# Gated attention and long convolution on one core: the convolution's operands are exchanged

## Chip, core and metric

The kernel runs on one core of a Trainium2 chip. The metric is device time in microseconds (us) of that core, from the first to the last instruction plus a small fixed part around it. Five engines work side by side, each through its own instruction stream in order: TensorE (PE), ScalarE (ACT), VectorE (DVE), GpSimd (POOL) and SyncE (SP, which here only starts DMA transfers). They meet at semaphores.

## The reference, cut to what matters

```python
S, D, H, Dh = 2048, 448, 16, 28          # one sequence
g = sigmoid((x * gate_w).sum(-1))         # one gate per position
q = (x @ wq).reshape(S, H, Dh); k = x @ wk; v = x @ wv      # one key and value for 16 heads
a = softmax(q k^T * Dh**-0.5) v  @ wo
dt = exp(log_dt)
K[d, l] = Re( sum_n C[d,n] * exp(dt[d] * A[d,n] * l) * dt[d] * B[d,n] )   # 256 complex modes
b[l, d] = sum_{m<=l} K[d, m] * u[l-m, d]  + u[l, d] * Dskip[d]            # by FFT in the reference
out = g * a + (1 - g) * b                 # A_x is both x and u
```

Attention has 16 x 2048 x 2048 exponentials. The second branch makes a filter K of 2048 taps for each of 448 channels and convolves it causally with x. All inputs and the output are bfloat16.

## The kernel before

**Attention.** There are 1024 score tiles of 128 keys by 512 (query, head) columns. They go through PSUM in sets of three and two: PE forms the scores (L1181), ACT takes the exponential of a whole set into a ring of 15 SBUF tiles (L1205), PE multiplies with the values (L1214) and accumulates 64 tiles in the bank psB. After 64 tiles `norm` moves psB to SBUF (`acc`, L1074 on ACT for the first 14 groups, L1076 on DVE for the next), gathers the denominators by three small DMAs of POOL (`denT`, `R_scratch`, `rdenB`) and multiplies on DVE (L1088). `outp` projects with wo and adds the result into O.

**Filter.** Channels come in 14 chunks of 32. For each chunk DVE builds tables of powers of the modes (`masters`, `tables`, L856 to L935), PE contracts them over the modes (`kgen`, L959), and the 64-column rows of taps are evacuated from PSUM: a DVE addition puts Dskip onto tap 0 (L969), an ACT copy moves the rest (L972). POOL then starts nine DMAs that write the taps reversed and padded into the DRAM scratch KP.

**Convolution.** A causal convolution is a product with a Toeplitz matrix. For four channels at a time `tload` (L996) reads KP with overlapping rows, each row starting one element after the one above, so that a DMA lays a Toeplitz tile of 128 partitions by 4288 columns (1072 KB) into SBUF. The partition index is 2m+h: m counts 64 shifts and h two halves of the sequence. There are 112 tiles, four for each of 28 half chunks; T has five buffers, and two further ones, in xT and tab, open for tiles 70 and 96 on. In `conv` PE holds columns of U stationary (x laid out by blocks of 64 positions and loaded once, 32-2n columns for step n, strided by the 448 channels) and streams 128 columns of the tile, with four channels side by side in four column groups (L1015). DVE scales the sum with 1-g (L1026), PE transposes it back (L1037), and DVE adds it into O (L1045).

**Order of the work.** The program is written as operations with what they read and write. `Prog.schedule` is a list scheduler: from estimated durations and priorities it picks the order of each engine's stream at build time[...]. A DMA is an operation of its issuing engine, with `free[e]` as its cost of issue (500 ns on SP, 1000 on POOL), `dmafree` as one shared transfer channel, and `extra` as added latency. `fill` then inserts matmuls with zeros into planned idle times of PE (L636, L640; L1187 in the score sets). `emit` writes waits for those dependencies that cross engines. The tile loads wait for the taps of their chunk in KP and for a free buffer; the convolution waits for its tile.

**What the change touches.** The constants NTR and `free[e]`; the buffers U, T, cst, dtb and the scratch KP in `alloc`; memsets in `consts`; the loads of U and the pad in `loads`; stores in `prep_x`; the last level in `masters`; the evacuation in `kgen`; `tload`; `conv`; and the copy at the head of `norm`.

Of the kernel before, what the change touches and what calls it, by code (L numbers as in the profile page):

```python
# [32 lines left out]
NTR = 5  # L33
# [47 lines left out]
class Prog:  # L81
# [65 lines left out]

    def schedule(self):
# [20 lines left out]
        while done < n:  # L169
# [55 lines left out]
            if o.slot is not None:  # L225
                free[e] = r + (1000.0 if e == "pool" else 500.0) * o.ndma
                s = r if e == "pool" else max(r, dmafree)
                end = s + o.ns + self.DMA_NS + o.extra
                dmafree = max(dmafree, s) + o.ns
            else:  # L230
                free[e] = r + o.ns
                end = free[e] + o.lat
# [124 lines left out]
class Kernel:  # L357
# [34 lines left out]
    def alloc(self):  # L392
# [23 lines left out]
        self.U = sb("U", D * 32, BF)  # L416
        self.O = sb("O", 16 * D, BF)
        self.T = sb("T", NTR * TW, BF)
        self.tslots = [(self.T, s * TW, ["tpdone", "rawdone"]) for s in range(NTR)]
        self.tslots.append((self.xT, NT * S - TW - 2048, [("xT", hp, q) for hp in range(2) for q in range(3)]))  # L420
        self.tmap, self.tlast = {}, [s - 9 for s in range(NTR)] + [-20, -20]
# [14 lines left out]
        self.cst = sb("cst", 512, BF)  # L436
# [4 lines left out]
        self.KP = nc.dram_tensor("KP_scratch", (2 * KH,), BF).ap()  # L441
# [4 lines left out]
    def consts(self):  # L446
# [6 lines left out]
        dm(V(self.kstg, 0, 256), 0.0, 170, [("kst", 0, 0), ("kst", 1, 0)])  # L453
# [10 lines left out]
        for k in range(2):  # L464
            dm(V(self.U, (16 + 8 * k) * D, 8 * D), 0.0, 1550, ["Uz"])
# [17 lines left out]
        dm(V(self.Wo, 0, NT * D), 0.0, 810, ["Wo"], 5)  # L483
        for q in range(4):
            dm(V(self.O, q * 4 * D, 4 * D), 0.0, 800, [("O", q)], 5)

    def loads(self):
# [14 lines left out]
        self.dtb = self.cst  # L502
# [21 lines left out]
        rs = self.U.rs  # L524
        for k, (h, p0, b0) in enumerate(((1, 16, 15), (0, 0, 15), (1, 0, 31))):
            ap = bass.AP(tensor=self.U.h, offset=h * rs + p0 * D, ap=[[2 * rs, 64], [D, 16], [1, D]])
            pg.dma([(ap, dram(x, 64 * b0 * D, [[D, 64], [-64 * D, 16], [1, D]]))],
                   (1024, 896), f"u{k}", rd=["Uz"] if p0 else [], wr=[("U", k)], pr=0.5)
        for k in range(2, 6):
# [6 lines left out]
        pg.dma([(dram(self.KP, KH + 1024, [[4 * KW, 112], [KW, 4], [1, 64]]), self.kstg.v(0, 112, 0, [[64, 4], [1, 64]]))],  # L536
               (448, 128), "pad", rd=[("kst", 0, 0), ("kst", 1, 0)], wr=["pad"], pr=3)
# [15 lines left out]
    def prep_x(self):  # L553
# [3 lines left out]
        for q in range(4):  # L557
# [43 lines left out]
            pg.op("pe", mv, 900, rd=["Wv", "Wvg"] + self.xk(q), wr=[("b", 6)], pr=0.5)  # L601
        pg.op("dve", lambda e: e.tensor_reduce(sm.v(0, P, 12, [[1, 1]]), sm.v(0, P, 8, [[1, 4]]), AX.X, ALU.max),
# [86 lines left out]
    def prep_gate(self):  # L689
# [11 lines left out]
        def mm(e):  # L701
            for mu in range(2):
                for par in range(2):
                    r = e.matmul(px.v(0, P, 64 * mu, [[1, 64]]), self.sel.v(0, 16, 128 * (1 + (1 - mu) - par), [[1, P]]),
                                 ogT.v(0, 16, 64 * par, [[1, 64]]), start=(par == 0), stop=(par == 1), tile_position=(0, 0),
                                 skip_group_check=True)
            return r
# [123 lines left out]
    def masters(self, b):  # L831
# [18 lines left out]
        def dv(fn, n, rd, wr, rate=0.96):  # L850
            pg.op("dve", fn, el(n, rate), rd=rd, wr=wr, pr=pr)
        two = lambda buf: buf.v(0, P, 0, [[BW, 2], [1, w]])
        one = lambda buf, comp: buf.v(0, P, comp * BW, [[1, w]])
        for k in range(11):
            if k:
                dv(lambda e, k=k: e.tensor_tensor(two(msq), both(k - 1), both(k - 1), ALU.mult), 2 * w, keys(k - 1), ["msq"])  # L856
                dv(lambda e, k=k: e.scalar_tensor_tensor(src(k, 1), src(k - 1, 0), 2.0, src(k - 1, 1), ALU.mult, ALU.mult),
                   w, keys(k - 1), ["sim"])
                dv(lambda e, k=k: e.tensor_tensor(src(k, 0), one(msq, 0), one(msq, 1), ALU.subtract), w, ["msq"], ["sre"])
# [11 lines left out]
        for lv in range(5):  # L871
            if lv:
                dv(lambda e: e.tensor_tensor(qq, qq, qq, ALU.mult), w, ["sqq"], ["sqq"])
            dv(lambda e, lv=lv: e.tensor_copy(mbf.v(0, P, 5 * MB + BW * lv, [[1, w]]), qq), w, ["sqq"] + tp, [("mq", lv)], 1.92)
# [63 lines left out]
    def kgen(self, c, sub=None):  # L938
# [13 lines left out]
        for jj in range(8):  # L952
            def mm(e, comp, jj=jj):
                for half in range(2):
                    for g in gs:
# [7 lines left out]
                            start=(comp == 0 and half == 0), stop=(comp == 1 and half == 1),  # L963
                            tile_position=(0, 32 * g), skip_group_check=True)
                return r
            for comp in range(2):
                pg.op("pe", lambda e, mm=mm, comp=comp: mm(e, comp), 226 if whole else 113, mode="c", st=2.08 if whole else 1.04,
                      rd=keys, wr=[X] + k1 + k2, pr=1.7, lock=G if jj == 0 and comp == 0 else None)
        pg.op("dve", lambda e: e.tensor_tensor(ko.v(p0, np, ks + 63, [[64, 8]]), G.v(p0, np, 63, [[64, 8]]),  # L969
                                               self.skt.v(p0, np, 8 * c, [[1, 8]]), ALU.add),  # L970
              el(8), rd=[X, "skt"], wr=k1, pr=2)
        pg.op("act", lambda e: e.activation(ko.v(p0, np, ks, [[64, 8], [1, 63]]), G.v(p0, np, 0, [[64, 8], [1, 63]]), AF.Copy),  # L972
              490, rd=[X] + k1, wr=k2, pr=-1, unlock=G)
        rs = ko.rs
        lst = [(dram(self.KP, (32 * c + 8 * gs[0]) * KW + 1024, [[8 * KW, len(gs)], [KW, 8], [1, 64]]),
                bass.AP(tensor=ko.h, offset=(p0 + 16) * rs + ks, ap=[[32 * rs, len(gs)], [64, 8], [1, 64]]))]
        for g in gs:
            for h in range(2):
                lst.append((dram(self.KP, h * KH + (32 * c + 8 * g) * KW, [[64, 16], [KW, 8], [1, 64]]),
                            ko.v(32 * g + 16 * h, 16, ks, [[64, 8], [1, 64]])))  # L980
        pg.dma(lst, (264 * len(gs), 128), f"kw{sub or 0}", rd=k1 + k2, wr=[("KP", 2 * c + h) for h in ((0, 1) if whole else (sub,))],
               pr=0, eng="pool", extra=2000)

# [7 lines left out]
    def tload(self, gi):  # L991
        pg = self.pg
        s = self.slot(gi)
        t, o, x = self.tslots[s]
        x, y = ([], x) if s >= NTR else (x, []) if gi < NTR else ([], [])
        pg.dma([(t.v(0, P, o, [[1, TW]]),  # L996
                 dram(self.KP, 4 * gi * KW, [[1, 64], [KH, 2], [1, TW]]))],
               (128, 2 * TW), f"T{s}", rd=[("KP", gi // 4), "pad"] + x, wr=[("T", s)] + y, pr=1, extra=2500)

    def conv(self, c):  # L1000
# [3 lines left out]
        ck, cx = ("cst", c % 2), [("xT", hp, 0) for hp in range(2)] if c == 1 else []  # L1004
        ps = self.grp()
        for k in range(4):
            self.tload(4 * c + k)
        for k in range(4):
# [3 lines left out]
            for n in range(8):  # L1012
                def mm(e, k=k, n=n, tb=tb, to=to, gi=gi):
                    for j in range(4):
                        r = e.matmul(ps.v(32 * j, 32 - 2 * n, 128 * k, [[1, 128]]),  # L1015
                                     self.U.v(0, P, 2 * n * D + 4 * gi + j, [[D, 32 - 2 * n]]),
                                     tb.v(0, P, to + j * KW + 896 - 128 * n, [[1, 128]]),
# [4 lines left out]
                pg.op("pe", mm, (94, 92, 90, 82, 76, 70, 58, 57)[n], st=1.54 - 0.0625 * n, mode="c", rd=[("T", s)] + [("U", q) for q in range(3)],  # L1022
# [4 lines left out]
                                               ps.v(0, P, 63, [[128, 4], [64, 2], [-1, 64]]),  # L1027
# [4 lines left out]
        def yt(e, k):  # L1032
            for par in range(2):
                for mu in (0, 1):
# [3 lines left out]
                                 cb.v(0, P, co + 128 * k + 64 * (1 - mu), [[1, 64]]),  # L1038
# [27 lines left out]
    def norm(self, i):  # L1066
# [6 lines left out]
        if i < 14:  # L1073
            pg.op("act", lambda e: e.activation(av, self.psB.v(0, P, 0, [[1, 512]]), AF.Copy), 490, rd=[("b", 6)], wr=[ak, kb], pr=-1)  # L1074
        elif i == 14:
# [224 lines left out]
```

## Time and profile before

| | before |
|---|---|
| median of 3 runs | 539.85 us (537.03 to 544.44) |
| profiled execution | 540.75 us, span 539.0 us |
| mean granted TensorE clock | 0.965 |
| busy: PE, DVE, ACT, POOL | 486.4, 449.5, 497.5, 102.1 us |
| DMA | 142.89 MB, 265 GB/s mean |

A page of the profile shows one execution. Its second part cuts the span into 40 slices of 13.5 us, each digit being tenths of busy time (9 is 90% or more); PEclk is the clock granted to TensorE. A group of instructions reads: line, engine, operation, what it writes and reads with shapes, count, then busy time in us and mean ns of one, then idle time of the engine just before them and what ended it. PEld is the load of a matmul's stationary operand. A line of windows reads: start and end in us, length, then busy time and count of PE, PEld, DVE, ACT and POOL, the granted clock, the mean busy share of the 16 DMA engines, and GB/s. The chain is the work that ended last, followed back from the end; its pieces give start, duration, engine, tile and line. A DMA issue line gives size and median us from issue to landing.

### The profile page before, as it was taken

Reading aid. Unit: us, or ns where it says so; the run is one execution under the profiler, and the core shown is the slowest. Engines: PE = TensorE matmul, PEld = TensorE weight load, DVE = VectorE, ACT = ScalarE, POOL = GpSimd, SP = SyncE. Lnnn points to the kernel's source line nnn. Section 1 sums busy time; section 2 is a strip of 40 time slices with the busy share of each in tenths; the row PEclk is TensorE's granted clock in tenths of the full one; section 3 lists DMA queues with packets and bytes.
Section 4 is the critical chain, followed back from the end, with each engine's and each line's share of the span. In section 5 each row is a group of like instructions: output and inputs, shape, how many; then the busy total and the mean of one; then the engine's idle time right before and its main releaser. Section 6 shows DMA issues by size and latency. Waiting matters only on the chain.

```text
span 539.0 us, 20180 instructions
## 1 busy us (share of the span) xinstructions
PE 486.4 (90%) x9186; PEld 249.5 (46%) x9186; DVE 449.5 (83%) x891; ACT 497.5 (92%) x458; POOL 102.1 (19%) x192
## 2 busy tenths in 40 slices
PE   7698999989999899888999898989999898999887
PEld 4442233235454555353555454553556355644434
DVE  7979999989999999899999999999999695331203
ACT  3799999998999999989999999999999796899992
POOL 2000002200431404012040430040042213220000
PEclk9989999998999999999999999999999796899998
DMA  8931100793398987979778989999859997999722
GB/s 235 283 121 47 37 21 7 251 347 116 118 376 300 329 358 284 351 259 386 296 240 363 327 273 348 400 351 367 343 191 356 353 380 287 348 344 392 261 88 71
DMA packets 39042, 142.89 MB, mean 265 GB/s; under 512 B 11240, under 2 KB 22032, under 8 KB 24620
## 3 DMA queue, kind: packets, MB, share of 16 engines
q1 hardware_dynamic: 28316, 135.30, 69.0%
q0 software_dynamic: 9104, 6.13, 4.4%
q8 instruction: 72, 1.18, 0.9%
q10 hardware_dynamic: 1536, 0.17, 0.3%
q14 instruction: 14, 0.11, 0.1%
HBM read 135.39 MB, written 5.74 MB: 262 GB/s over the span
## 4 chain that ended last, share of the span: by engine, by line
ACT 56%; PE 26%; DMA 8%; DVE 8%; issue 2%; ACTq 0%
ACT expT L1205 54%; PE psS L1181 7%; PE psB L1214 4%; PE psS L959 3%; PE psX L959 3%; DMA rdenB<-R_scratch 3%; PE psX L1015 3%; DMA denT<-acc 2%; DMA sz<-in_A_wv_dram 2%; PE psS L1015 2%; ACT acc L1074 1%; DMA R_scratch<-denT 1%; DVE msq L856 1%; DVE xT L576 1%; DVE tab L911 1%
## 5 line engine op out<-in xcount | busy, mean ns | idle before, releaser
L1205 ACT ACTIVATE expT<-psS 128x1536 bf16<-128x1536 f32 (+1 forms) x410 | 470.6, 1340 | 18.7 <-PE psS L1181 11.7
L1181 PE MATMUL psS<-qT,kT 32*128 32x512 bf16 x1024 | 164.3, 395 | 29.8 <-ACT expT L1205 22.3
L1214 PE MATMUL psB<-expT,vaug 128*32 128x512 bf16 x1024 | 105.1, 400 | 3.7 <-issue 3.2
L1181 PEld LDWEIGHTS psS<-qT,kT 32*128 32x128 bf16 x1024 | 39.5, 91 | 119.3 <-ACT expT L1205 97.3
L1187 PE MATMUL psB<-ident,zero 32*128 32x512 bf16 x190 | 74.9, 394 | 0.0
L911 DVE TENSOR_TENSOR tab<-tab,mbf 128x256 bf16<-128x256 bf16 (+5 forms) x75 | 69.6, 928 | 1.2
L1015 PE MATMUL psX<-T,U 128*18 128x128 bf16 (+7 forms) x1920 | 54.7, 243 | 4.2 <-issue 3.2
L1214 PEld LDWEIGHTS psB<-expT,vaug 128*32 128x32 bf16 x1024 | 26.4, 93 | 64.8 <-issue 62.8
L1015 PEld LDWEIGHTS psX<-T,U 128*18 128x18 bf16 (+7 forms) x1920 | 47.6, 161 | 15.1 <-issue 11.2
L640 PE MATMUL psB<-ident,zero 128*32 128x512 bf16 (+3 forms) x728 | 48.6, 336 | 0.0
L138 POOL DMA_DIRECT2D KP_scratch<-xT x64 | 34.4, 544 | 43.6 <-ACT xT L972 43.6
L138 POOL DMA_DIRECT2D KP_scratch<-kstg x63 | 34.1, 549 | 34.2 <-ACT kstg L972 32.5
L959 PE MATMUL psX<-tab 128*32 128x64 bf16 x960 | 39.7, 293 | 0.3 <-DVE tab L935 0.3
L913 DVE TENSOR_TENSOR tmp<-tab,mbf 128x256 bf16<-128x256 bf16 (+4 forms) x62 | 39.6, 638 | 0.0
L1015 PE MATMUL psS<-T,U 128*32 128x128 bf16 (+7 forms) x1344 | 39.3, 243 | 0.0
L138 POOL DMA_DIRECT2D denT<-acc x15 | 10.8, 717 | 146.8 <-ACT acc L1074 137.9
L1015 PEld LDWEIGHTS psS<-T,U 128*32 128x32 bf16 (+7 forms) x1344 | 34.0, 161 | 8.9 <-issue 6.9
L959 PE MATMUL psS<-tab 128*32 128x64 bf16 x832 | 35.3, 293 | 0.0
L138 POOL DMA_DIRECT2D R_scratch<-denT x15 | 8.6, 576 | 138.7 <-DVE denT L1082 59.2
L930 DVE TENSOR_TENSOR tab<-tab,tmp 128x2048 bf16<-128x2048 bf16 x28 | 33.5, 1219 | 0.2
L959 PEld LDWEIGHTS psX<-tab 128*32 128x32 bf16 x960 | 30.3, 138 | 6.7 <-issue 3.8
L959 PEld LDWEIGHTS psS<-tab 128*32 128x32 bf16 x832 | 26.4, 137 | 7.4 <-issue 5.4
(179 smaller groups left out, 599.1 us busy)
## 6 DMA issues: line engine op xcount, KB each, us to landing
T<-KP_scratch SPq DMA_DIRECT2D x102, 1072.0 KB, 11.0
xT<-KP_scratch SPq DMA_DIRECT2D x7, 1072.0 KB, 10.5
rdenB<-R_scratch POOLq DMA_DIRECT2D x15, 256.0 KB, 12.4
tab<-KP_scratch SPq DMA_DIRECT2D x3, 1072.0 KB, 8.8
U<-in_A_x_dram SPq DMA_DIRECT2D x3, 896.0 KB, 15.4
tab<-in_A_x_dram SPq DMA_DIRECT2D x4, 448.0 KB, 7.5
SZ_scratch<-tab SPq DMA_DIRECT2D x1, 1344.0 KB, 8.6
out_dram<-O SPq DMA_DIRECT2D x3, 448.0 KB, 3.8
```

The costliest lines, as they stand in the source:

```text
L138: return [e.dma_start(o, i, **kw) for o, i in pairs]
L576: pg.op("dve", lambda e, d=dst, s=src: e.tensor_copy(d, s), 1130, rd=[("b", b)], wr=[key], pr=-0.6)
L640: r = e.matmul(t.v(32 * j, 32, bo, [[1, 128 * m]]), self.zero.v(0, P, 0, [[1, 32]]), self.ident.v(0, P, 0, [[0, m], [1, P]]), start=not ac ...
L911: vo(lambda e, dst=dst, src=src, mr=mr: e.tensor_tensor(dst, src, mr, ALU.mult), 2 * n, done + mk(lv), kr + ki)
L913: vo(lambda e, src=src, mi=mi, w=w, n=n, tb=tb, to=to: e.tensor_tensor(tb.v(0, P, to, [[n, 2], [cw, w], [1, cw]]), src, mi, ALU.mult), 2 * ...
L930: vo(lambda e, h=h: e.tensor_tensor(tab.v(0, P, FM + 32 * h, [[64, 2], [EW, 32], [1, 32]]), tab.v(0, P, lo + 31 * EW + 64 * h, [[BLK, 2], ...
L959: r = e.matmul(G.v(32 * g, 32, 64 * jj, [[1, 64]]), tab.v(0, P, lo + comp * BLK + 32 + o, [[EW, 32]]), tab.v(0, P, fo, [[mo - fo, 2], [EW, ...
L1015: r = e.matmul(ps.v(32 * j, 32 - 2 * n, 128 * k, [[1, 128]]), self.U.v(0, P, 2 * n * D + 4 * gi + j, [[D, 32 - 2 * n]]), tb.v(0, P, to + j ...
L1181: r = e.matmul(self.psS.v(0, P, 512 * (bo + k), [[1, 512]]), kT.v(32 * h, 32, 128 * kt, [[1, 128]]), qT.v(32 * h, 32, 512 * (i % 2), [[1, ...
L1187: r = e.matmul(self.psB.v(0, P, 0, [[1, 512]]), self.zero.v(32 * h, 32, 0, [[1, P]]), self.ident.v(32 * h, 32, 0, [[0, 4], [1, P]]), start ...
L1205: pg.op("act", lambda e: e.activation(expT.v(0, P, 512 * es, [[1, n]]), self.psS.v(0, P, 512 * bo, [[1, n]]), AF.Exp, scale=SQ), 50 + n / ...
L1214: r = e.matmul(self.psB.v(32 * h, 32, 0, [[1, 512]]), vaug.v(0, P, 32 * kt, [[1, 32]]), expT.v(0, P, 512 * (t % RING), [[1, 512]]), start= ...
```

## The change

The convolution is symmetric in filter and signal, and the two change places.

- x, transposed, is stored once into a DRAM scratch XP (with 64 zeros ahead), and the 112 Toeplitz tiles are read from it. A tile's partition is now 64h+m, and it is loaded by two DMAs of 64 partitions. The tiles don't depend on the filter.
- The taps of a chunk become the stationary operand. ACT copies all 512 columns; Dskip is added before that by four small matmuls (`tap`). POOL stores the taps into a DRAM scratch K2 by eight DMAs, and SP brings them back by two transposing DMAs of 128 by 512 into Ku, which holds two chunks.
- U goes, and T has eight buffers. Four of them are not shared with the raw parameters. A load waits for the tile load three ahead of it.
- The accumulator copies of `norm` for groups 0 to 13 go from ACT to DVE.
- Smaller edits: memsets of Wo and O go from DVE to POOL; two levels of `masters` write their last result straight to bf16; cst and dtb share other buffers; the scheduler's cost of an issue is 250 and 550 ns.

```diff
-NTR = 5
+NTR = 8
@@ Prog
+    def tdma(self, out, inp, slot, rd, wr, pr):
+        o = self.dma([(out, inp)], (128, 1024), slot, rd, wr, pr, extra=1500)
+        o.fn = lambda e: [e.dma_start_transpose(out, inp)]
@@ schedule
-                free[e] = r + (1000.0 if e == "pool" else 500.0) * o.ndma
+                free[e] = r + (550.0 if e == "pool" else 250.0) * o.ndma
@@ alloc
-        self.U = sb("U", D * 32, BF)
+        self.Ku = sb("Ku", 2 * 1024, BF)
-        self.tslots = [(self.T, s * TW, ["tpdone", "rawdone"]) for s in range(NTR)]
+        self.tslots = [(self.T, s * TW, ["tpdone", "rawdone"] if s < 4 else []) for s in range(NTR)]
-        self.cst = sb("cst", 512, BF)
+        self.cst = Sub(self.xT, 1024)
-        self.KP = nc.dram_tensor("KP_scratch", (2 * KH,), BF).ap()
+        self.XP = nc.dram_tensor("XP_scratch", (2 * KH,), BF).ap()
+        self.K2 = nc.dram_tensor("K2_scratch", (2 * 1024 * P,), BF).ap()
@@ consts
-        dm(V(self.kstg, 0, 256), 0.0, 170, [("kst", 0, 0), ("kst", 1, 0)])
-        for k in range(2):
-            dm(V(self.U, (16 + 8 * k) * D, 8 * D), 0.0, 1550, ["Uz"])
-        dm(V(self.Wo, 0, NT * D), 0.0, 810, ["Wo"], 5)
+        pm(V(self.Wo, 0, NT * D), 0.0, 1000, ["Wo"], 5)
         for q in range(4):
-            dm(V(self.O, q * 4 * D, 4 * D), 0.0, 800, [("O", q)], 5)
+            pm(V(self.O, q * 4 * D, 4 * D), 0.0, 1000, [("O", q)], 5)
@@ loads
-        rs = self.U.rs
-        for k, (h, p0, b0) in enumerate(((1, 16, 15), (0, 0, 15), (1, 0, 31))):
-            ap = bass.AP(tensor=self.U.h, offset=h * rs + p0 * D, ap=[[2 * rs, 64], [D, 16], [1, D]])
-            pg.dma([(ap, dram(x, 64 * b0 * D, [[D, 64], [-64 * D, 16], [1, D]]))],
-                   (1024, 896), f"u{k}", rd=["Uz"] if p0 else [], wr=[("U", k)], pr=0.5)
...
+        for b in range(2):
+            pg.dma([(dram(self.K2, b * 1024 * P + 16 * P + 64, [[32 * P, 32], [P, 16], [1, 64]]), self.zero.v(0, 32, 0, [[0, 16], [1, 64]]))],
+                   (512, 128), "kz", rd=["zero"], wr=[("K2", b, h) for h in range(2)], pr=3)
...
@@ prep_x
+            lst = [(dram(self.XP, (q // 2) * KH + 64 + 512 * (q % 2), [[KW, DT], [DT * KW, 4], [1, 512]]),
+                    xT.v(0, DT, 2048 * q, [[512, 4], [1, 512]]))]
+            if q == 1:
+                lst.append((dram(self.XP, KH, [[KW, DT], [DT * KW, 4], [1, 64]]), xT.v(0, DT, 2048 + 448, [[512, 4], [1, 64]])))
+            pg.dma(lst, (448, 1024), "xp", rd=self.xk(q), wr=[("XP", q)], pr=0.6)
@@ masters
+                if k == 10:
+                    dv(lambda e: e.scalar_tensor_tensor(last(1), f[0], 2.0, f[1], ALU.mult, ALU.mult), w, keys(9) + tp, [("mb", 10)])
+                    dv(lambda e: e.tensor_tensor(last(0), f[2], f[3], ALU.subtract), w, ["msq"] + tp, [("mb", 10)])
+                    continue
...
+            if lv == 4:
+                dv(lambda e: e.tensor_tensor(mbf.v(0, P, 5 * MB + BW * 4, [[1, w]]), qq, qq, ALU.mult), w, ["sqq"] + tp, [("mq", 4)])
+                continue
@@ kgen
-        pg.op("dve", lambda e: e.tensor_tensor(ko.v(p0, np, ks + 63, [[64, 8]]), G.v(p0, np, 63, [[64, 8]]),
-                                               self.skt.v(p0, np, 8 * c, [[1, 8]]), ALU.add),
-              el(8), rd=[X, "skt"], wr=k1, pr=2)
-        pg.op("act", lambda e: e.activation(ko.v(p0, np, ks, [[64, 8], [1, 63]]), G.v(p0, np, 0, [[64, 8], [1, 63]]), AF.Copy),
-              490, rd=[X] + k1, wr=k2, pr=-1, unlock=G)
+        def tap(e):
+            for g in gs:
+                r = e.matmul(G.v(32 * g, 32, 63, [[64, 8]]), self.ident.v(0, P, 32 * g, [[1, 32]]), self.skt.v(0, P, 8 * c, [[1, 8]]),
+                             start=False, stop=True, tile_position=(0, 32 * g), skip_group_check=True)
+            return r
+        pg.op("pe", tap, 113 if whole else 57, mode="c", st=0.7 if whole else 0.35, rd=["skt", "id"], wr=[X], pr=1.6)
+        pg.op("act", lambda e: e.activation(ko.v(p0, np, ks, [[1, 512]]), G.v(p0, np, 0, [[1, 512]]), AF.Copy),
+              490, rd=[X], wr=k1 + k2, pr=-1, unlock=G)
...
         for g in gs:
+            for h, m0 in ((0, 0), (1, 16)):
+                lst.append((dram(self.K2, kb + 8 * g * 32 * P + 64 * h, [[P, 32 - m0], [32 * P, 8], [1, 64]]),
+                            ko.v(32 * g + m0, 32 - m0, ks, [[64, 8], [1, 64]])))
+        pg.dma(lst, (384 * len(gs), 128), f"kw{sub or 0}", rd=k1 + k2, wr=[("K2", c % 2, h) for h in hs],
                pr=0, eng="pool", extra=2000)
+        for h in hs:
+            o = self.Ku.v(0, P, 1024 * (c % 2) + 512 * h, [[512, 1], [1, 512]])
+            i = dram(self.K2, kb + 512 * h * P, [[P, 512], [1, P]])
+            pg.tdma(o, i, f"kt{c % 2}{h}", rd=[("K2", c % 2, h)], wr=[("Ku", c % 2, h)] + (["dt"] if c < 2 else []), pr=0)
@@ tload
-        pg.dma([(t.v(0, P, o, [[1, TW]]),
-                 dram(self.KP, 4 * gi * KW, [[1, 64], [KH, 2], [1, TW]]))],
-               (128, 2 * TW), f"T{s}", rd=[("KP", gi // 4), "pad"] + x, wr=[("T", s)] + y, pr=1, extra=2500)
+        pg.dma([(t.v(64 * h, 64, o, [[1, TW]]), dram(self.XP, h * KH + 4 * gi * KW + 1, [[1, 64], [1, TW]])) for h in range(2)],
+               (128, 2 * TW), f"T{s}", rd=[("XP", q) for q in range(4)] + ["pad"] + x, wr=[("T", s)] + y, pr=1, extra=1500)
+        o = pg.ops[-1]
+        self.tops.append(o.i)
+        if len(self.tops) > 3:
+            o.deps[self.tops[-4]] = 1
@@ conv
-                                     self.U.v(0, P, 2 * n * D + 4 * gi + j, [[D, 32 - 2 * n]]),
-                                     tb.v(0, P, to + j * KW + 896 - 128 * n, [[1, 128]]),
+                                     self.Ku.v(0, P, ku + 32 * (4 * k + j) + 2 * n, [[1, 32 - 2 * n]]),
+                                     tb.v(0, P, to + j * KW + 128 * n, [[1, 128]]),
...
-                pg.op("pe", mm, (94, 92, 90, 82, 76, 70, 58, 57)[n], st=1.54 - 0.0625 * n, mode="c", rd=[("T", s)] + [("U", q) for q in range(3)],
+                pg.op("pe", mm, (94, 92, 90, 82, 76, 70, 58, 57)[n], st=1.54 - 0.0625 * n, mode="c", rd=[("T", s), ("Ku", c // 2 % 2, c % 2)],
@@ norm
-        if i < 14:
-            pg.op("act", lambda e: e.activation(av, self.psB.v(0, P, 0, [[1, 512]]), AF.Copy), 490, rd=[("b", 6)], wr=[ak, kb], pr=-1)
-        elif i == 14:
+        if i < 15:
             pg.op("dve", lambda e: e.tensor_copy(av, self.psB.v(0, P, 0, [[1, 512]])), el(512), rd=[("b", 6)], wr=[ak, kb], pr=0)
```

## The prediction, made before the changed kernel was run

> **What bounds the kernel now.** First the page: busy times, the slices, the chain that ended last.
>
> ```profile
> span 539.0 us, 20180 instructions
> PE 486.4 (90%) x9186; PEld 249.5 (46%) x9186; DVE 449.5 (83%) x891; ACT 497.5 (92%) x458; POOL 102.1 (19%) x192
> ...
> PEclk9989999998999999999999999999999796899998
> DMA  8931100793398987979778989999859997999722
> ...
> ACT 56%; PE 26%; DMA 8%; DVE 8%; issue 2%; ACTq 0%
> ```
>
> ACT, which takes the exponentials, is fullest. PE holds a quarter of the chain, and its granted clock dips where DMA stands at 9. Next the groups by line and shape, and the DMA issues:
>
> ```profile
> L1205 ACT ACTIVATE expT<-psS 128x1536 bf16<-128x1536 f32 x205 | 318.4, 1553 | 12.6 <-PE psS L1181 11.7 <-PE psB L1187 0.7
> L1214 PEld LDWEIGHTS psB<-expT,vaug 128*32 128x32 bf16 x1024 | 26.4, 93 | 64.8 <-issue 62.8 <-ACT acc L1074 1.2 <-ACT expT L1205 0.7
> L1015 PEld LDWEIGHTS psX<-T,U 128*32 128x32 bf16 x240 | 11.1, 166 | 5.0 <-issue 3.1 <-DVE qT L828 1.3 <-DVE xT L1026 0.2
> L1074 ACT ACTIVATE acc<-psB 128x512 f32<-128x512 f32 x14 | 8.7, 621 | 0.2 <-PE psB L1214 0.2
> ...
> T<-KP_scratch SPq DMA_DIRECT2D x102, 1072.0 KB, 11.0
> ```
>
> Then 20 us windows, and the chain in order of time:
>
> ```profile
> 100.00:120.00 20.00, 18.31 (x317) 7.39 (x317) 18.42 (x48) 20.00 (x19) 0.89 (x2) 1.00 1.01 359
> 420.00:440.00 20.00, 17.99 (x326) 9.07 (x330) 15.59 (x34) 16.57 (x16) 1.24 (x2) 0.83 0.99 361
> 440.00:460.00 20.00, 18.30 (x348) 10.74 (x352) 13.21 (x35) 15.74 (x15) 6.46 (x12) 0.71 0.85 312
> 480.00:500.00 20.00, 18.62 (x378) 9.47 (x375) 4.38 (x9) 20.00 (x19) 1.29 (x2) 1.00 1.00 373
> ...
> 418.72 2.65 issue
> ...
> 471.63 56.11 ACT expT L1205 x50
> ```
>
> The last line shows the exponentials undisturbed: 56.11/50 = 1.122 us each, so 410 need 460.2 us. Before the first one 26.7 us pass, after the last about 10.8. The 14 accumulator copies (L1074) hold the chain for some 0.5 us each (0.49 at 59.84), 7.0 in all; the 15 evictions of taps (L972) likewise, 7.3. That makes 512.0; the other 27 us are stalls. About 9 fall in 420 to 470 us: 50 less 34 exponentials at 1.122, less three evictions and two copies at 0.5, leaves 9.3. There DMA is full, PE stands for 2.65 us (an "issue" gap: no work of another engine is named), and ACT waits.
>
> [...] after the gap at 418.72 the 512-wide matmuls take 0.61 us for 0.39. [...] The stationary U columns are 896 bytes apart; their weight loads take 166 ns against 93 for contiguous columns of equal shape. [...] 128-partition tiles run at 359 to 373 GB/s. [...]
>
> **The change, part by part**, against the profiled 540.75 us (span 539.0 and 1.75 around it; the median of the runs is 539.85, so the two agree).
>
> *Accumulator copies.* ACT loses 14, −7.0 us. VectorE takes them at 0.60 us in its stream (0.69 by the one of L1076), +8.4. Other VectorE edits: two U memsets 3.1, five of Wo and O 4.05, 15 Dskip additions (L969) at about 0.15 = 2.2, staging memset 0.17, and four blocks' last-level casts and copies some 0.4+0.3 each = 2.8; together −12. VectorE gets no fuller. PE's next accumulation waits in order behind the copy, and queries and keys queue behind that; ACT used to answer promptly (1.2 us of such waits in all), while a VectorE table operation may run 2.3 us. The rings of exponentials and the two score sets hide most. Bounds 0 and 14×1.1 (half a table operation) = 15; I take +3.
>
> *Start.* The chain crosses two O memsets of 0.81 us before the first exponential: −1.6. On POOL the five cost 14 times the 0.20 us of the 128-wide memset, 14 us in all, under its idle stretch from 20 to 60 us; without that cover O's first use at 124 us still leaves room. The U loads (2.7 MB) go; five XP stores of 1.8 MB and three of zeros come on SP, behind the x loads, some 8×0.5 us of issue while SP has nothing urgent; the staging for odd and even chunks moves into spent columns of xT, read last by 60 us. All zero.
>
> *Eviction of taps.* One ACT copy without the VectorE addition ahead of it: the 2.1 us that ACT waited there (three times) go; −2. The tap matmuls, 60 with eight columns, at about 25 ns as in the convolution (35 in 0.89 us) are 1.5 us of PE, spread over 14 chunks; zero to +1.5, I take 0, as PE has filler beside it.
>
> *Weight loads.* The 3584 convolution matmuls keep their shapes, and their stationary becomes contiguous. If loads set the pace, the chain's 4.4% on L1015 (24 us) shrinks by 1−93/166 = 0.44, at most −10; if the moving side does, 0. PE is seldom last: −3.
>
> *Taps through DRAM.* POOL issues 8 stores a chunk for 9 (0.55 us each: −0.5 us on POOL), then SP two transposes of 128 KB, 28 or so in all. [...] with three tiles at 3 us ahead in the rings, 15 us. Before, a tile came 10.6 us (median) after the taps had landed, so the delay is −5 to +10. It shifts chunks, which are two-buffered, not the rate: taken as 0. A transpose waiting for the stores blocks the tile loads behind it in SP's queue; eight loaded buffers are its cover.
>
> *Tiles.* They no longer wait for taps; eight can be there by 108 us, when the convolution now starts. I take −5 of the 9 us at 420 to 470, as loads spread into the empty slices at 40 to 95 us (bounds −9 and 0); next late is ACT itself. What each load costs is the open term: two DMAs of 64 partitions for one of 128, an extra SP issue of 0.51 us (112 more, 57 us on an idle queue). The new wait of each load for the one three tiles ahead of it (at most three in flight) holds SP, with transposes and output stores queued behind; at 3 us a tile that is 9 us of queue against the 10.6 us a tile took to land before, so nobody waits longer: 0. At today's 1.098 MB/0.365 = 3.0 us a tile all is hidden.
>
> Sum: −7 +3 −1.6 −2 −3 −5 = −15.6, so 525 us; 513 to 538 with the bounds.
>
> **The rivals.** *B, the half loads bind.* [...] The convolution takes tiles from 108 to 518 us; eight are there at its start, and 104 loads share the 410 us with other DMA (142.9 MB in all less 122.9 of tiles, about half of it after the start: some 40 us), so a tile may take 370/104 = 3.6 us. Above this the load stream sets the end[...]. [...] Against it: the halves follow each other in one queue[...]. Slower, 565 to 690, 625 in the middle.
>
> *C, the copies bind.* VectorE is 97% busy from 60 to 420 us. If its order slips against PE's, each of 14 copies costs 1.1 us and every second one a clock dip with some 2 us of ACT, as between 120 and 140 us: 14×(1.1+1.0) = 29 on the rest of the sum, −18.6: 551. Against: VectorE sheds as much as it gets.
>
> *D, the gain is given back.* Copies leave ACT, and PE, which holds a quarter of the chain, is what it then waits for; stalls under full DMA stay. Then start and evictions are all that is left: 537.
>
> **How the numbers follow.** A (forecast, 525) 0.48; B 0.34; C 0.08; D 0.10. A alone ranges 513 to 538, three quarters under 529. A measurement tells 2% from no change, that is 529 to 551. Faster: 0.36+0.01 = 0.37; within 2%: 0.12 of A, 0.09 of D, half of C: 0.25; slower: B and half of C, 0.38. The range runs from 513 to 615 and leaves out the slower half of B.
>
> **What would show it.** Right: L1074 gone from ACT, ACT still first, weight loads of the convolution near 95 ns, DMA share filled between 40 and 95 us, full clock at 420 to 470. B: DMA share near 1.0 throughout[...], PE idle ahead of convolution matmuls. C: PE waiting for VectorE's acc copies for over 10 us. Wrong above all: if the halves need more than 3.6 us a tile.

## The result and the profile after

| | before | after |
|---|---|---|
| median | 541.87 us (537.03 to 544.44, 4 runs) | 766.36 us (762.41 to 770.62, 4 runs) |
| span of the profiled execution | 539.0 us | 765.3 us |
| mean granted TensorE clock | 0.965 | 0.767 |
| busy: PE, DVE, ACT, POOL | 486.4, 449.5, 497.5, 102.1 us | 564.1, 455.5, 504.1, 104.0 us |
| DMA | 142.89 MB, 265 GB/s mean | 146.73 MB, 192 GB/s mean |

The ratio is 1.416, with a 95% interval of 1.402 to 1.430. Here and below, ratios and their intervals leave out executions that took over 1.5% longer than the fastest of their kernel, while medians and ranges keep them. The kernel is 225 us slower, far outside the range of 513 to 615 us. The parts of the page after that answer to those shown before are the busy times, the slices (of 19.1 us here) and the chain:

```profile
span 765.3 us, 20612 instructions
PE 564.1 (74%) x9310; PEld 243.3 (32%) x9310; DVE 455.5 (60%) x874; ACT 504.1 (66%) x444; POOL 104.0 (14%) x182
...
PEclk9999997967778886857776777668685875855867
DMA  9349939944999999999999999999999999999993
GB/s 246 117 132 216 216 67 211 222 82 103 184 218 201 203 202 204 227 204 189 219 200 214 184 226 204 209 224 204 181 226 183 225 203 212 228 134 215 203 215 115
...
DMA 44%; PE 27%; DVE 9%; issue 8%; ACT 7%; SPq 4%; POOL 1%
```

The DMA row is at 9 from the eleventh slice to the last but one, and the row below says what it moves there: 181 to 228 GB/s in all of these slices but one. The engines' row of nines has become a DMA row of nines. ACT, which held 56% of the chain before, has 7%. Next the groups by line and the DMA issues:

```profile
L1229 ACT ACTIVATE expT<-psS 128x1536 bf16<-128x1536 f32 (+1 forms) x410 | 481.9, 1270 | 222.8 <-PE psS L1205 178.0
L1041 PE MATMUL psX<-T,Ku 128*32 128x128 bf16 (+7 forms) x1664 | 51.0, 253 | 63.8 <-DMA T<-XP_scratch 23.5
...
L1100 DVE COPY acc<-psB 128x512 f32<-128x512 f32 x15 | 10.3, 689 | 53.6 <-PE psB L1238 53.6
...
T<-XP_scratch SPq DMA_DIRECT2D x210, 536.0 KB, 14.7
```

The exponentials (now L1229) take about what they took (481.9 us for 470.6). Of the 222.8 us of idle time before them all but some 19 are new, and 178.0 end with score matmuls. In PE's stream scores stand behind convolution steps (L1041), before which PE was idle for 41.8 us until a tile landed and for 27.4 until taps did. One such step: PE stands for 2.71 us until a tile lands and goes on at 323.45 us, the next score matmuls start at 323.62, and ACT, which has waited 2.78 us for them, goes on at 324.28. A last view, windows (start, end and length in us; busy time and count of PE, PEld, DVE, ACT, POOL; granted clock; DMA share; GB/s), after and then before:

```profile
360.00:380.00 20.00, 12.44 (x297) 7.02 (x295) 12.85 (x17) 12.32 (x11) 4.99 (x9) 0.84 1.00 214
500.00:520.00 20.00, 14.33 (x251) 5.82 (x248) 12.60 (x22) 11.20 (x10) 1.73 (x4) 0.67 1.02 223
```

```profile
360.00:380.00 20.00, 17.82 (x314) 8.21 (x315) 18.29 (x31) 18.15 (x17) 2.54 (x5) 0.91 0.96 366
```

With equally full DMA engines the rate is 214 to 223 GB/s for 366. The tile is as large as it was, and is moved at some 0.6 of the speed. As the engines are full (1.00 and 1.02), this is a rate and not a delay. Two small readings show how it reaches the rest. The chain between 282 and 333 us holds almost only tiles:

```profile
282.34 17.62 DMA T<-XP_scratch
...
300.46 18.02 DMA T<-XP_scratch
...
318.98 14.38 DMA T<-XP_scratch
```

Each piece is a load of SP that waits for the load three ahead of it: with three in flight, 16.7 us a piece are 5.6 us a tile. And a transfer that has nothing to do with the tiles pays too: at 147.51 us a reload of 384 KB for the next masters goes out among the tile loads and takes 14.79 us, in which VectorE waits 12.0 us for it. The median of the three such reloads is 16.1 us, for 3.7 in the kernel before.

### The profile page after: what moved, and what is told of

The parts are those of the page before. It is cut to its first block, busy times and chain, and to the rows that moved or that the text cites. A ratio compares the mean times of both kernels' runs of the same rounds, so it can differ in the third digit from the quotient of the medians.

```text
span 765.3 us, 20612 instructions
## 1 busy us (share of the span) xinstructions
PE 564.1 (74%) x9310; PEld 243.3 (32%) x9310; DVE 455.5 (60%) x874; ACT 504.1 (66%) x444; POOL 104.0 (14%) x182
## 2 busy tenths in 40 slices
DMA packets 55845, 146.73 MB, mean 192 GB/s; under 512 B 29376, under 2 KB 37936, under 8 KB 41420
## 4 chain that ended last, share of the span: by engine, by line
DMA 44%; PE 27%; DVE 9%; issue 8%; ACT 7%; SPq 4%; POOL 1%
DMA T<-XP_scratch 25%; PE psS L1205 8%; DMA Ku<-K_scratch 6%; ACT expT L1229 6%; PE psB L1238 5%; DMA xT<-XP_scratch 5%; DMA rdenB<-R_scratch 2%; PE psS L1041 2%; PE psX L974 2%; PE psS L974 2%; SPq L138 2%; SPq L150 2%; PE psX L1041 2%; DMA sz<-SZ_scratch 2%; DMA K_scratch<-kstg 2%
## 5 line engine op out<-in xcount | busy, mean ns | idle before, releaser
L1229 ACT ACTIVATE expT<-psS 128x1536 bf16<-128x1536 f32 (+1 forms) x410 | 481.9, 1270 | 222.8 <-PE psS L1205 178.0
L1205 PE MATMUL psS<-qT,kT 32*128 32x512 bf16 x1024 | 195.4, 472 | 14.8 <-ACT expT L1229 6.2
L1238 PE MATMUL psB<-expT,vaug 128*32 128x512 bf16 x1024 | 125.5, 479 | 1.6 <-DVE acc L1100 1.6
L1041 PE MATMUL psX<-T,Ku 128*32 128x128 bf16 (+7 forms) x1664 | 51.0, 253 | 63.8 <-DMA T<-XP_scratch 23.5
L1041 PE MATMUL psS<-T,Ku 128*20 128x128 bf16 (+7 forms) x1696 | 50.9, 255 | 52.7 <-issue 32.9
L1211 PE MATMUL psB<-ident,zero 32*128 32x512 bf16 x190 | 88.9, 468 | 0.0
L974 PE MATMUL psX<-tab 128*32 128x64 bf16 x960 | 42.4, 295 | 26.3 <-issue 16.7
L1041 PEld LDWEIGHTS psX<-T,Ku 128*32 128x32 bf16 (+7 forms) x1664 | 33.6, 107 | 83.9 <-issue 34.8
L1041 PEld LDWEIGHTS psS<-T,Ku 128*32 128x32 bf16 (+7 forms) x1696 | 34.5, 107 | 72.0 <-issue 46.8
L861 DVE TENSOR_TENSOR msq<-sz 128x512 f32<-128x512 f32 (+1 forms) x40 | 24.8, 620 | 28.3 <-DMA sz<-SZ_scratch 28.2
L138 POOL DMA_DIRECT2D K_scratch<-kstg x56 | 30.9, 560 | 72.1 <-ACT kstg L990 71.1
L138 POOL DMA_DIRECT2D K_scratch<-xT x56 | 31.0, 561 | 39.5 <-ACT xT L990 31.7
## 6 DMA issues: line engine op xcount, KB each, us to landing
T<-XP_scratch SPq DMA_DIRECT2D x210, 536.0 KB, 14.7
```

Of the source, the lines that this page charges most:

```text
L138: return [e.dma_start(o, i, **kw) for o, i in pairs]
L974: r = e.matmul(G.v(32 * g, 32, 64 * jj, [[1, 64]]), tab.v(0, P, lo + comp * BLK + 32 + o, [[EW, 32]]), tab.v(0, P, fo, [[mo - fo, 2], [EW, ...
L1205: r = e.matmul(self.psS.v(0, P, 512 * (bo + k), [[1, 512]]), kT.v(32 * h, 32, 128 * kt, [[1, 128]]), qT.v(32 * h, 32, 512 * (i % 2), [[1, ...
L1211: r = e.matmul(self.psB.v(0, P, 0, [[1, 512]]), self.zero.v(32 * h, 32, 0, [[1, P]]), self.ident.v(32 * h, 32, 0, [[0, 4], [1, P]]), start ...
L1229: pg.op("act", lambda e: e.activation(expT.v(0, P, 512 * es, [[1, n]]), self.psS.v(0, P, 512 * bo, [[1, n]]), AF.Exp, scale=SQ), 50 + n / ...
L1238: r = e.matmul(self.psB.v(32 * h, 32, 0, [[1, 512]]), vaug.v(0, P, 32 * kt, [[1, 32]]), expT.v(0, P, 512 * (t % RING), [[1, 512]]), start= ...
```

## The experiments

**Theories.** *P, partitions*: DMAs of 64 adjacent partitions move at a lower rate than those of 128, whatever is queued beside them, and the load stream sets the end. This is the prediction's rival B. The 5.0 us a tile and 218 GB/s of the expectations below lie between what the two windows above make of a tile of 1.098 MB: 5.1 us at 214 GB/s, 4.9 at 223. *N, number*: twice as many DMAs of half the size cost the rate, by their issue or their fixed part. *R, transposes*: the 28 transposing DMAs stall the rings. *C, copies*: the accumulator copies on VectorE delay PE's next accumulation. The diffs are cut to the lines that matter; where the order is to stay although the number of DMAs changes, the line that keeps the planner's cost is left out.

### The kernel before, with halves of adjacent and of alternating partitions

The tile load of the kernel before, first as two DMAs of 64 adjacent partitions, then as two DMAs of every second partition. Both compute the whole reference, and every engine but SP has the order of the kernel before.

```diff
-        pg.dma([(t.v(0, P, o, [[1, TW]]), dram(self.KP, 4 * gi * KW, [[1, 64], [KH, 2], [1, TW]]))],
# adjacent
+        pg.dma([(t.v(64 * z, 64, o, [[1, TW]]), dram(self.KP, 4 * gi * KW + 32 * z, [[1, 32], [KH, 2], [1, TW]])) for z in range(2)],
# alternating
+        pg.dma([(bass.AP(tensor=t.h, offset=z * rs + o, ap=[[2 * rs, 64], [1, TW]]), dram(self.KP, z * KH + 4 * gi * KW, [[1, 64], [1, TW]])) for z in range(2)],
```

> The kernel before, its tile load cut into two DMAs of 64 adjacent partitions (0 to 63, 64 to 127); the order of every engine is unchanged. Theory P[...]: tile rate near 218 GB/s, 5.0 us a tile, DMA share near 1 from 100 us to the end, 112 tiles x 5.0 + 97 + 21 = 680 us, 650 to 720. Theory N (two DMAs of half the size cost more, whatever their partitions): as in the run with alternate partitions, 560 to 600 in both. Theory X (transposes, instruction fetch and SP's queue are what costs): 540 to 550.

> The kernel before, its tile load cut into two DMAs of 64 alternate partitions (even, odd), so each spans all 128; the order of every engine is unchanged. Theory P: no loss, 540 to 552 us, tile rate still over 330 GB/s in full windows. Theory N: the same time as the run with adjacent halves. Theory X: 540 to 550.

Adjacent: 741.9 us (one run; the kernel before took 539.41 beside it). Alternating: 537.83 us, a ratio of 0.9995 (0.9963 to 1.0027). Slices and issue line of the adjacent halves, and then of the alternating ones:

```profile
GB/s 251 215 38 23 18 155 207 160 137 223 214 221 220 234 214 221 209 221 210 217 227 209 226 209 224 234 225 225 205 184 215 213 224 227 216 230 219 221 79 100
...
T<-KP_scratch SPq DMA_DIRECT2D x204, 536.0 KB, 19.6
```

```profile
GB/s 236 284 126 43 42 22 7 233 339 152 116 359 324 328 368 218 348 326 344 360 211 388 313 279 356 391 343 357 389 210 279 378 371 344 328 362 403 288 56 107
...
T<-KP_scratch SPq DMA_DIRECT2D x204, 536.0 KB, 8.9
```

Number, size, planned issue cost and bytes are the same in the two. What differs is the partitions that one DMA covers, and with them which rows of the source it reads; but the changed kernel's loads read the source as the alternating halves do, 64 shifts of one half of the sequence, and are slow, so the partitions remain. One has 205 to 234 GB/s in all slices but one from 185 us to 703, the other up to 403. N is refuted. P is shown, and alone it is worth 202 of the 225 us; how adjacent partitions come to the lower rate no run shows.

### The changed kernel with full tiles, with plain taps, and with both

Each tile by one DMA of 128 partitions, and the transposing DMAs as plain ones of the same bytes, one at a time and together. The orders and sizes are those of the changed kernel. What these kernels leave out is the right second branch: with full tiles the rows meet the wrong taps, and plain taps come untransposed.

```diff
# full tiles
-        pg.dma([(t.v(64 * h, 64, o, [[1, TW]]), dram(self.XP, h * KH + 4 * gi * KW + 1, [[1, 64], [1, TW]])) for h in range(2)],
+        pg.dma([(t.v(0, P, o, [[1, TW]]), dram(self.XP, 4 * gi * KW + 1, [[1, 64], [KH, 2], [1, TW]]))],
# plain taps
-        o.fn = lambda e: [e.dma_start_transpose(out, inp)]
+        o.fn = lambda e: [e.dma_start(out, inp)]
...
-            i = dram(self.K2, kb + 512 * h * P, [[P, 512], [1, P]])
+            i = dram(self.K2, kb + 512 * h * P, [[512, P], [1, 512]])
```

> The changed kernel, each tile loaded by one DMA of 128 partitions in the old row order 2m+h; the order of every engine is unchanged. Rows are thereby paired with the wrong taps, so the second branch is not computed as in the reference; all sizes stay. Theory P: 150 us or more of the 225 come back, 540 to 610 us, the rest being transposes. Theory N: the same. Theory X: 720 us or more. Against the run with alternate partitions it tells P from N.

> The changed kernel, the two transposing DMAs of a chunk replaced by plain DMAs of the same bytes (128 rows of 1 KB); the order of every engine is unchanged. The taps come untransposed, so the second branch is not computed as in the reference. Theory P: tile loads still bind at 5.0 us, 112 x 5.0 + 40 + about 100 = 690 to 740 us. Theory X: most of the 225 us come back, under 620 us.

> The changed kernel with tiles of 128 partitions in one DMA (rows paired with the wrong taps) and the transposing DMAs replaced by plain ones of the same bytes (taps untransposed), so the second branch is not computed as in the reference; the order of every engine is that of the changed kernel. Tile loads no longer bind. Theory T (the transposes hold the rings, and with them PE's instruction fetch): 10 us or more come back from the 551 with transposes, 530 to 541. Theory V (the accumulator copies on VectorE cost what is left): still 546 to 553.

| | time, us | against before | T lands in | Ku lands in |
|---|---|---|---|---|
| after | 766.36 | 1.416 | 14.7 us | 15.2 us |
| plain taps | 735.58 (one run) | – | 13.4 us | 15.5 us |
| full tiles | 551.24 (543.0 to 552.8) | 1.020 (1.002 to 1.039) | 9.0 us | 4.4 us |
| both | 544.05 (541.6 to 550.3) | 1.013 (1.005 to 1.021) | 9.1 us | 3.8 us |

The chain with full tiles, and the tile's issue line:

```profile
ACT 41%; PE 24%; DMA 16%; DVE 14%; issue 4%; POOL 0%; POOLq 0%
...
T<-XP_scratch SPq DMA_DIRECT2D x105, 1072.0 KB, 9.0
```

One DMA for two takes 215 us off the changed kernel. ACT leads the chain again, with 41% (53% with plain taps too). Plain taps take 31 us off while the tiles bind (one run, but four runs of the changed kernel lie within 9 us) and 4 us by the ratios when they don't, which the overlapping intervals don't resolve. So R seems real, on one run, and is the smaller part. Where the transposes may hurt is a window that follows two of them, which SP issued from 234 to 245 us, in the changed kernel:

```profile
248.00:255.00 7.00, 0.06 (x6) 0.01 (x2) 0.46 (x1) 0.76 (x1) 0.00 (x0) 0.78 1.03 157
```

All engines stand for nearly all of the 7 us, with a DMA share of 1.03 and the rate at 157 GB/s. The chain puts 6.94 us there down to PE's own issue, in the middle of a group of matmuls: no work of another engine is named. Such waits of PE add up to 76.6 us in the changed kernel, 47.8 with plain taps, 31.3 in the kernel before with adjacent halves and 7.8 in the kernel before as it was. So they come with the slow tiles, and the transposes add to them. Instructions come by DMA too (the page has a queue for them, of 1.2 MB), so a fetch that stood behind full queues would fit, but no run tried it.

### Full rate with the change's own partition order

To have one DMA and the right order, the source can run over the halves outside and the shifts inside.

```diff
-        pg.dma([(t.v(64 * h, 64, o, [[1, TW]]), dram(self.XP, h * KH + 4 * gi * KW + 1, [[1, 64], [1, TW]])) for h in range(2)],
+        pg.dma([(t.v(0, P, o, [[1, TW]]), dram(self.XP, 4 * gi * KW + 1, [[KH, 2], [1, 64], [1, TW]]))],
```

> The changed kernel with a single edit: each tile is loaded by one DMA of all 128 partitions whose source runs over the two halves of the sequence outside and the 64 shifts inside, so that every row lands in the partition where the change puts it. Nothing of the computation is left out; the engines' orders are those of the changed kernel. If what costs is which partitions one DMA covers, the rate goes back to some 360 to 400 GB/s, a tile lands in 9 to 12 us and the time is that of the full tiles with mispaired rows, 551 us (543 to 555). Rival: a source whose outermost dimension is only 2 is handed to the DMA engines half by half, so that the upper partitions follow the lower ones inside one DMA: then the rate stays near 215 GB/s and the time near 740 to 770 us.

Measured: 2449.3 us (2447.8 to 2450.5), 4.54 times the kernel before. Neither 551 nor 740 to 770; both expectations missed. A window of this kernel:

```profile
500.00:520.00 20.00, 1.04 (x32) 0.77 (x32) 3.79 (x9) 0.00 (x0) 0.00 (x0) 0.50 0.13 54
```

The mean share of the 16 DMA engines is 0.13, which is that of two engines at work (2/16), and 54 GB/s are moved, 27 for each. In 24 of the 40 slices the DMA row is at 1, and where it is higher the rate is not (0.50 and 59 GB/s from 2000 to 2020 us). So a load with an outermost dimension of 2 ran as if on two engines; with the 64 shifts outermost, in the kernel with full tiles, the same bytes went at 376 GB/s from 180 to 200 us and 315 from 320 to 340. The change's two DMAs of 64 partitions avoid this and meet 0.6 of the rate instead. A version without the wait for the load three ahead was run with the same load:

```diff
-        if len(self.tops) > 3:
-            o.deps[self.tops[-4]] = 1
```

> As the run with one DMA for a tile, and without the rule that a tile load waits for the third load ahead of it, so that the eight buffers may be filled as soon as they are free; the planner's order changes with it. Nothing is left out. If that rule holds loads back once the rate is whole again, waits of the chain for T (5% of the chain before, 16% of it for tiles and denominators with full tiles) shrink and the time falls by 4 to 10 us against the run with the rule. If the rate was all, the two are within 1%. If deep prefetch stands in the way of the small denominator gathers and the taps, it is 3 to 10 us slower.

2456.01 us: as slow as with the wait, it says nothing of the wait at full rate, and that stays open (its order differs too).

### The halves through two queues

The upper half of every tile comes from POOL's queue, the lower from SP's, in a new order of the planner; the whole reference is computed.

```diff
+        pg.dma([(t.v(64, 64, o, [[1, TW]]), src(1))], (64, 2 * TW), f"V{s}", rd=rdx + x, wr=[("V", s)] + y, pr=1, eng="pool", extra=1500)
+        pg.dma([(t.v(0, 64, o, [[1, TW]]), src(0))], (128, 2 * TW), f"T{s}", rd=rdx + x, wr=[("T", s)] + y, pr=1, extra=1500)
```

> The changed kernel, the upper half of each tile loaded from GpSimd's queue, the lower half from SyncE's. Theory P[...]: with two queues the halves can be in flight at once[...]; if they fall out of step the tile rate rises to 290 GB/s or more and the time to 580 to 640 us. If engines stay in step, as in one queue, 218 GB/s and 740 to 790 us.

826.69 us (one run). The slices of 20.6 us and the issue lines:

```profile
GB/s 235 103 162 234 144 33 236 224 33 178 176 214 189 204 157 203 204 173 167 168 215 195 183 179 202 186 179 159 187 188 128 152 198 197 154 192 186 222 213 165
...
T<-XP_scratch SPq DMA_DIRECT2D x105, 536.0 KB, 14.1
T<-XP_scratch POOLq DMA_DIRECT2D x105, 536.0 KB, 14.8
```

Two queues don't bring the rate back; no slice is above 236 GB/s. The chain has 22% in the three denominator transfers (before, 8% for all DMA together), whose issues now stand in POOL's queue among tile loads, before which POOL waits up to 19.4 us at a time (140.9 us in all) for convolution matmuls. But ACT's row is empty from 660 us on, and the slices from the tenth on have 128 to 222 GB/s, where the changed kernel has 181 to 228 in its full ones. So the load stream sets the end here too, and a lower rate fits the 60 us by which this kernel is worse. Why two halves in two queues don't add up, and why they are slower still, was not settled.

### The copies, alone and taken back

The kernel before with its first 14 accumulator copies on VectorE and nothing else, and the changed kernel with full tiles and these copies back on ACT (the same lines the other way round). Both have a new order.

```diff
# before, copies on VectorE
-        if i < 14:
-            pg.op("act", lambda e: e.activation(av, self.psB.v(0, P, 0, [[1, 512]]), AF.Copy), 490, rd=[("b", 6)], wr=[ak, kb], pr=-1)
-        elif i == 14:
+        if i < 15:
             pg.op("dve", lambda e: e.tensor_copy(av, self.psB.v(0, P, 0, [[1, 512]])), el(512), rd=[("b", 6)], wr=[ak, kb], pr=0)
```

> The kernel before with one part of the change alone: the accumulator copies of groups 0 to 13 on VectorE instead of ScalarE; the scheduler makes a new order. By the prediction's term ScalarE loses 7 us and waits cost 3: 4 us faster, 534 to 538. Theory V (PE waits behind the copies, and the clock dips): 545 to 560.

> The changed kernel with tiles of 128 partitions in one DMA (rows paired with the wrong taps, so the second branch is not computed as in the reference), the accumulator copies of groups 0 to 13 on ScalarE again; the scheduler makes a new order. Theory T: 551 as with the copies on VectorE, or up to 7 us more, since ScalarE gets 7 us of work back. Theory V: 535 to 545.

The first gave 547.97 us, a ratio of 1.0146 (1.0079 to 1.0213); the second 558.15, 1.0355 (1.0306 to 1.0403), against 551.24 and 1.020 with the copies on VectorE. From the waits and the chain of the first:

```profile
ACT O L1151 <- PE psS L1138: 20.7, 2, 20.5
```

```profile
519.10 12.01 DMA T<-KP_scratch
```

ACT is 7.8 us less busy than before, and its exponentials end at about 518 us for 528. But then the last tile is still to come: it lands at 531, and ACT waits 20.5 us for the last sums. The gain on ACT became a wait at the end. Something delayed the convolution: the last tile's load is issued at 519.1 us for 497.8, once PE frees its buffer. VectorE, which got 9.7 us busier, starts its last addition for the tables at 468.4 us for 461.4, and the last taps leave PSUM at 477.7 for 470.4. So the copies seem to have pushed back the tables from which the taps are made, though the new order may have its part in it: in the second run the copies left VectorE, and that kernel is slower too. The same move costs 1.5% in one kernel and gains 1.5% in the other, so the two settle no price. C is wrong: PE's matmuls wait 1.2 us for VectorE's copies in this run, and in the changed kernel 1.6 us (2.5 for the weight loads beside them).

### The small edits alone

The kernel before with memsets of Wo and O on POOL and the masters' last level straight to bf16; then the same with the tap matmuls and the single ACT copy as well. The edits are the lines of the change.

```diff
-        dm(V(self.Wo, 0, NT * D), 0.0, 810, ["Wo"], 5)
+        pm(V(self.Wo, 0, NT * D), 0.0, 1000, ["Wo"], 5)
-            dm(V(self.O, q * 4 * D, 4 * D), 0.0, 800, [("O", q)], 5)
+            pm(V(self.O, q * 4 * D, 4 * D), 0.0, 1000, [("O", q)], 5)
# the second also
...
+        pg.op("pe", tap, 113 if whole else 57, mode="c", st=0.7 if whole else 0.35, rd=["skt", "id"], wr=[X], pr=1.6)
```

> The kernel before with two of the small edits only: memsets of Wo and O on GpSimd, and the last level of both master sets written straight to bf16. The taps' eviction stays an addition on VectorE and a copy of 504 columns on ScalarE; nothing is left out. With these and the four small matmuls and the 512-column copy the kernel was 1.28% slower than before. If the exchange of the eviction costs that, this run is back at the time of the kernel before (ratio 0.995 to 1.003) or at my 1.6 us of gain. If any new order that the planner makes costs about as much, it stays 0.5 to 1.5% slower.

> The kernel before with the small edits of the change alone: memsets of Wo and O on GpSimd, the last level of both master sets written straight to bf16, and the Dskip addition on VectorE replaced by four small matmuls and one copy of 512 columns on ScalarE. Tiles, taps in KP, U and the accumulator copies stay as they are; nothing is left out. My sum gave these a gain of 1.6 us at the start plus about 2 us for the taps' eviction: 536 us (532 to 540) beside 540. Rival: these lie beside other work and the order that the planner makes of them moves the time by up to 1% either way: 540 to 546 us.

The first gave 550.39 us, 1.019 (1.012 to 1.027); the second 550.40 us, 1.013 (1.009 to 1.016). The masters and memsets were meant to save time and the first is slower by 1 to 3%. With the eviction's edits added it is not slower still, so these are not the cause. What all six kernels at full rate whose streams stand in another order than those of the kernel before have in common is that they are slower: the two with full tiles, the one with the copies taken back, the one with the copies alone and these two lie at 1.013 to 1.036. The first one's clock row shows where some of its time goes:

```profile
PEclk9989999999999999999999999999959967578999
```

Each digit is 13.7 us, so the granted clock is down to 0.5 to 0.7 from 440 to 495 us (and in one slice at 399), and from 440 us on ACT waits 13.7 us for score matmuls. Its last tile is late too: the load is issued at 515.8 us, in the second run at 512.9, for 497.8 before. That the order as such costs the 1 to 3%, rather than some edit in it, is argued from the likeness of the six and was not shown: undoing one edit changes the order too.

## Why the prediction was wrong, point by point

- **What bounds the kernel now** stands: with full tiles the chain has ACT first again. But with the tiles put right the kernel takes 551 us where 525 was forecast, 2% more than before and not 3% less, so the gains of the sum fail as well. (Its bounds for copies, weight loads and tiles also add up to 511 to 545, not to 513 to 538.)
- **Tiles, the step that failed.** "At today's 1.098 MB/0.365 = 3.0 us a tile all is hidden" took the rate of a 128-partition load for a load in two halves. The halves run at 181 to 228 GB/s in full slices, a load every 6.1 us on average (112 tiles, issued from 51.3 to 734.3 us), above the 3.6 us from which rival B said the load stream decides. The adjacent and alternating halves in the kernel before show the cause. The reason against B, that the halves follow each other in one queue, did not save the rate: no full slice of the changed kernel is above 228 GB/s, and none in the stream of the adjacent halves above 234.
- **Rival B** named the cause and stood at 34 in 100; its size was low. What a half tile takes, on which its times rest, was not shown by the trace before. Measured, 5.0 us a tile and the 40 us for other DMA fit the adjacent halves in the kernel before: 112 tiles were issued in 586 us (97.2 to 683.4), and 112×5.0 + 40 is 600. In the changed kernel three terms were missing: the transposes, 31 us; the rings were partly idle from 96 to 115 us and from 153 to 191 (67, 82 and 103 GB/s in these slices), the second time after VectorE's tables had waited for their reload; and reloads that queue with tiles, 12 us of VectorE for one of them. The middle of 625 and the upper end of the range, 615, counted on less than that price, which no trace showed. With the time of the new load not measured and so little against it, the rival deserved more than 34 in 100.
- **The rate of the halves.** In full windows of 20 us the adjacent halves show 218 and 225 GB/s and the changed kernel 214 and 223, against 338 to 377 in the kernel before: a ratio of about 0.6. Two DMAs for a tile's adjacent halves show no gain, in one queue or in two: no full slice is above 228 GB/s in the changed kernel, none above 236 with two queues. The trace before has only tiles of 128 partitions, and the prediction forecast the halves at that rate.
- **Taps through DRAM**, "taken as 0": wrong by one run, in which the transposes cost 31/28 = 1.1 us each while the rings are full; beside loads at full rate it is some 4 us in all, not resolved from nothing. What a transpose takes was not shown by the trace before, which has none.
- **Accumulator copies**, −7 +3: both sizes were near (ACT 7.8 us less busy in the kernel before with that edit alone, PE's waits 2 us), the sum's sign was not. The prediction counted ACT's gain on the whole as time, though it had itself listed 10.8 us of work after the last exponential. The last tile became late (its load 21 us later than before), and the kernel with this edit alone is 1.5% slower. The prediction set against C that VectorE sheds as much as it gets. In the whole change it nearly does (451.8 us busy with full tiles for 449.5); alone the copies made it 9.7 us busier, and its last tables came 7 us later. Rival C, 14 waits of 1.1 us with clock dips, is refuted by the waits just given.
- **Start and eviction**, −1.6 and −2: not found. The kernels with these edits alone are 1.9% (start) and 1.3% (both) slower.
- **Weight loads**: 95 ns median with contiguous columns for about 160 with columns 896 bytes apart, near the 93 predicted. In time no run isolates them; where the tiles bind they can't count.
- **The wait for the load three ahead**, 0: it is what SP waits for most in the changed kernel (285.5 us), but at 0.6 of the rate it only shows the rate. With full tiles SP still waits 147.4 us for it. Its own price is open.
- **What would make the prediction wrong** was right: it was the rate of two half loads.

## What to carry to other kernels

Which partitions one DMA covers was part of its price: two DMAs of 64 adjacent partitions moved the same bytes at 0.6 of the rate (214 to 225 GB/s for 338 to 377), two of every second partition lost nothing (361 and 367), and one whose outermost dimension is 2 ran as if on two of 16 engines (a share of 0.13, 54 GB/s). Before a layout is swapped for its arithmetic, work out per tile what the new load takes at its new shape, compare with the time that the loop leaves for a tile, and look at the DMA share together with GB/s, since full queues at 0.6 of the rate show the same row of nines. And a gain on the leading engine counts only so far as what ends after it moves too: the last tile, here, stood 12 us in its way.

## What the runs showed of the hardware that was not expected

- Halves of adjacent partitions, queued behind each other over 500 us, stay at 205 to 234 GB/s but for one slice of 184, and a second queue doesn't help (128 to 222 in the slices from the tenth on). Halves of alternating partitions reach 403.
- A load with an outermost dimension of 2 showed the share of two DMA engines (0.13 of 16, 54 GB/s from 500 to 520 us), and took the kernel to 2449 us.
- Transposing DMAs between loads that fill the queues cost more than plain ones of the same bytes: 31 us for 28 of them by one run. SP took 1.1 to 9.8 us to issue one (median 1.8), and 0.4 to 2.7 (median 0.6) for a half tile of 536 KB. After two of them the rate fell to 157 GB/s for 7 us from 248 us on, and PE stood for 6.94 us amid a group of matmuls; that the transposes caused this is not shown.
